# A new order of steps for a windowed-attention and gated-MLP kernel with a hand-written list of steps

## The chip, the core and the metric

The kernel runs on one core of a Trainium2 chip. Such a core has four engines that compute, each with its own queue that is worked off strictly in order: TensorE (PE in the profile; PEld is its loading of weights), VectorE (DVE), ScalarE (ACT) and GpSimd (POOL). SyncE (SP) issues transfers. The engines wait for each other by semaphores. The metric is the device time of one execution in microseconds, lower is better; the time before is the median of 13 runs.

## What is computed

Attention over 4 batches, 8 heads, 768 positions and heads of 64, where a position sees itself, the 127 before it and the first 4 ("sinks"); then a gated MLP with a mixing over positions, and a residual:

```
scores = where(is_sink | in_window, q @ k.T / sqrt(64), -1e9)
x      = softmax(scores) @ v                       # heads side by side: [4, 768, 512]
h      = gelu_tanh(x @ w_in)                       # 512 -> 1024
u, v   = halves of h
v_n    = (v - mean) / sqrt(var + 1e-6) * g_ln
v_s    = einsum('ts,bsd->btd', w_sg, v_n) + b_sg   # mixes positions, 768 x 768
out    = x + (u * v_s) @ w_out                     # 512 -> 512
```

Inputs and output are float32; the kernel computes in bfloat16 and accumulates in float32.

## The kernel before

The whole program is a list of names, `STEPS`. Each name calls a short function that emits the instructions of one step; the loop at the end of the kernel goes through the list under a manual schedule. So **the list is the order of every engine's queue**: an engine gets its instructions in the order in which the steps that use it stand. The waits between engines follow from the data and from the reuse of buffers. A last letter D, A or P says which engine does a step that several could do (VectorE, ScalarE, GpSimd).

```python
        for step in STEPS.split():
            name, *idx = step.split(".")
            done[step] = code[name](*(int(i) if i.isdigit() else i for i in idx))
```

The steps, with b the batch, p the pair of heads (0 to 3), and the lines of the profile:

- **Loads.** LQ, LK, LV (L192, L196, L214) are issued by GpSimd and cast to bfloat16; a batch of q or k comes in 4 parts for batches 0 and 3 and in 2 parts for batches 1 and 2. LW, LWS, LWO are the weights (L233, L237, L240). A buffer of q or k holds two parts (`q16`, `k16`: ring of 2), so that a later load waits until TQ or TK has read the earlier one.
- **Turning q and k.** TQ, TK (L300) turn a pair's q or k on TensorE, 12 transposes on half the array's columns; EQ, EK (L219 on ScalarE, L221 on VectorE) copy the result out of PSUM. For batch 3, EQ and EK are instead transposing transfers issued by SyncE (L310), and XD (L427) does the same with x for batches 2 and 3.
- **Attention.** QK.b.p.g (L350) computes scores of group g of two key tiles (g = 0, 1, 2; the last is smaller), 4 matmuls on half the array's rows; EX (L358, ScalarE) is exp; MK (L365 on VectorE as a product with a mask, L369 and L373 on GpSimd as two selects) masks; KS (L323), SK (L332, L336) and SX (L341) make the sinks' weights. AV.b.p.half (L390, L396, L400) multiplies with v, with a column of ones for the sum; it needs the masks of groups 0 and 1 (half 0) or 1 and 2 (half 1). NR (L409, L410, VectorE) divides by the sum and writes x.
- **MLP.** XT (L419) and XE (L219, L221) turn x; MV (L436) and GV (L440) make the half that is normalised, MU (L478) and GU (L484) the other. BN, RS, NM (L449, L457, L460) are the statistics, Z (L466 on ScalarE, L469 on VectorE) normalises. WT and WE (L491, L494) turn the mixing weights. SP (L499) mixes positions, GT (L504, VectorE) scales and adds the bias, GM (L509 on VectorE or GpSimd) multiplies with u, OU (L516) is the last product, RA (L520) adds x, ST (L523) stores.
- **HM.n** puts n filler matmuls (L180) ahead of the next step on TensorE; they write to the PSUM buffer that this step is about to overwrite.

PSUM is two rings: `sc` of 2 double buffers for QK, MV and MU, and `mm` of 4 for everything else. A step on TensorE thus also waits for the reader of the buffer two or four uses back. The mask step shows how a step chooses its engine:

```python
    def MK(b, p, g, e="D"):
        ...
        if e == "D":
            m = (mask0 if g == 0 else mask1)[:, 0:w]
            nc.vector.tensor_mul(pt[:, :, 0:w], pt[:, :, 0:w],
                                 m.unsqueeze(1).to_broadcast([128, 2, w]))
            return
```

In the list, attention of the next batch is interleaved with the MLP of the one before; the list ends with the MLP of batch 3 alone.

Of the kernel before, what the change touches and what calls it, by code (L numbers as in the profile page):

```python
# [25 lines left out]
WT.3 WE.2 WT.5 GV.0.1 MV.0.2 WE.3 BN.0.0 MU.0.0 GV.0.2 WE.5 BN.0.1 WT.0 GU.0.0 MU.0.1 BN.0.2 RS.0.1 WT.4 GU.0.1 TQ.1.1
TQ.1.0 EQ.1.1.A MU.0.2 LQ.2.0 WE.4 EQ.1.0.A NM.0.1 RS.0.2 WE.0 Z.0.3.A MU.0.3 Z.0.0.D Z.0.1.A NM.0.2 Z.0.4.D Z.0.2.A
TK.1.0 Z.0.5.D WT.1 GU.0.3 EK.1.0.D SP.0.1.0 GU.0.2 WE.1 SP.0.1.2 GT.0.1.0 GM.0.1.0.P QK.1.0.1 GT.0.1.2 QK.1.0.0
TQ.1.2 EX.1.0.1 GM.0.1.2.D TQ.1.3 EQ.1.2.D SP.0.1.3 SP.0.0.2 GT.0.1.3 EQ.1.3.A MK.1.0.1.D TK.1.3 EX.1.0.0 GM.0.1.3.D
TK.1.2 GT.0.0.2 QK.1.0.2 EK.1.2.A SP.0.1.1 EK.1.3.D GM.0.0.2.P EX.1.0.2 QK.1.2.2 MK.1.0.0 SP.0.0.3 EX.1.2.2 MK.1.0.2.D  # L30
GT.0.1.1 QK.1.2.0 QK.1.3.0 GT.0.0.3 EX.1.2.0 TQ.2.0 GM.0.1.1.P TK.1.1 EQ.2.0.D SP.0.0.1 EX.1.3.0 LK.2.0 MK.1.2.0
LV.2.0 EK.1.1.A QK.1.2.1 GM.0.0.3.D QK.1.3.2 OU.0.5 EX.1.2.1 GT.0.0.1 LV.2.1 KS.1.0 OU.0.3 EX.1.3.2 RA.0.5 MK.1.2.1.P
SK.1.0 RA.0.3 ST.0.5 QK.1.3.1 SX.1.0 LQ.2.1 QK.1.1.2 MK.1.3.2.D TQ.2.1 ST.0.3 AV.1.0.1 MK.1.3.0 LK.2.1 EQ.2.1.A
AV.1.0.0 MK.1.2.2.D LV.2.2 AV.1.2.0 NR.1.0.1 EX.1.3.1 AV.1.2.1 NR.1.0.0 GM.0.0.1.P TK.2.1 EX.1.1.2 QK.1.1.0 NR.1.2.1
TK.2.0 MK.1.3.1.P EK.2.1.A QK.1.1.1 NR.1.2.0 EX.1.1.0 LV.2.3 MK.1.1.2.D AV.1.3.1 EX.1.1.1 MK.1.1.0 QK.2.1.2 LQ.3.0
AV.1.3.0 NR.1.3.1 EX.2.1.2 OU.0.4 NR.1.3.0 EK.2.0.A MK.1.1.1.P QK.2.1.1 RA.0.4 QK.2.1.0 EX.2.1.1 XT.1.3 LK.3.0 XT.1.1
ST.0.4 XE.1.3.D AV.1.1.0 EX.2.1.0 TQ.2.3 XE.1.1.D AV.1.1.1 NR.1.1.0 LV.3.0 EQ.2.3.A QK.2.0.2 MK.2.1.0 QK.2.0.1 TQ.2.2
EX.2.0.2 LQ.3.1 NR.1.1.1 TK.2.3 EQ.2.2.A TK.2.2 EK.2.3.D XT.1.2 EK.2.2.A LK.3.1 XT.1.0 XE.1.2.D QK.2.0.0 EX.2.0.1
SP.0.0.0 KS.2.0 LV.3.1 EX.2.0.0 XE.1.0.D SK.2.0 GT.0.0.0 MV.1.0 LQ.3.2 SX.2.0 MK.2.0.0 GM.0.0.0.D EQ.3.0 MK.2.0.1.D
OU.0.1 MK.2.0.2.P GV.1.0 AV.2.0.0 RA.0.1 MK.2.1.2.P MV.1.1 MK.2.1.1.P ST.0.1 EK.3.0 BN.1.0 MV.1.2 GV.1.1 BN.1.1  # L40
AV.2.1.1 GV.1.2 EQ.3.1 OU.0.2 BN.1.2 OU.0.0 RS.1.1 MU.1.3 LK.3.2 EK.3.1 RA.0.0 MU.1.1 NM.1.1 GU.1.3 RA.0.2 LV.3.2
Z.1.3.A Z.1.0.D MU.1.2 NR.2.1.1 RS.1.2 GU.1.1 ST.0.2 ST.0.0 NR.2.0.0 LQ.3.3 MU.1.0 GU.1.2 Z.1.1.D EQ.3.2 NM.1.2
Z.1.2.D LK.3.3 AV.2.0.1 Z.1.4.D GU.1.0 Z.1.5.D QK.2.2.0 AV.2.1.0 NR.2.0.1 EX.2.2.0 LV.3.3 SP.1.1.3 NR.2.1.0 SP.1.0.1
GT.1.1.3 EK.3.2 GM.1.1.3.D QK.2.2.1 GT.1.0.1 QK.2.3.0 SP.1.0.0 EX.2.2.1 MK.2.2.0 GM.1.0.1.P EX.2.3.0 SP.1.1.1 GT.1.0.0
MK.2.2.1.P QK.2.3.1 GT.1.1.1 QK.2.2.2 SP.1.1.0 EX.2.3.1 GM.1.0.0.D EQ.3.3 GM.1.1.1.D MK.2.3.0 EX.2.2.2 AV.2.2.0
QK.2.3.2 MK.2.3.1.D SP.1.0.3 EX.2.3.2 NR.2.2.0 MK.2.2.2.P EK.3.3 AV.2.3.0 GT.1.1.0 QK.3.1.2 QK.3.1.0 GT.1.0.3
GM.1.1.0.P AV.2.2.1 EX.3.1.2 NR.2.3.0 SP.1.1.2 EX.3.1.0 GM.1.0.3.P NR.2.2.1 XD.2.0 QK.3.0.0 MK.2.3.2.D QK.3.0.2
SP.1.0.2 EX.3.0.0 GT.1.1.2 KS.3.0 EX.3.0.2 AV.2.3.1 GT.1.0.2 GM.1.1.2.P SK.3.0 NR.2.3.1 QK.3.0.1 SX.3.0 QK.3.1.1
OU.1.4 MK.3.0.2.D EX.3.0.1 XD.2.1 GM.1.0.2.D MK.3.1.0 OU.1.3 EX.3.1.1 MK.3.0.1.D OU.1.2 MK.3.1.1.D MU.2.1 RA.1.4
RA.1.2 MV.2.0 ST.1.4 RA.1.3 GU.2.1 ST.1.2 MK.3.1.2.D ST.1.3 MK.3.0.0 OU.1.1 GV.2.0 MV.2.1 RA.1.1 BN.2.0 ST.1.1 MV.2.2  # L50
GV.2.1 BN.2.1 MU.2.3 GV.2.2 OU.1.5 BN.2.2 RS.2.1 GU.2.3 OU.1.0 MU.2.0 NM.2.1 RS.2.2 RA.1.0 Z.2.3.A RA.1.5 ST.1.0
MU.2.2 Z.2.2.D GU.2.0 ST.1.5 NM.2.2 Z.2.1.D Z.2.0.D AV.3.1.0 GU.2.2 QK.3.3.2 Z.2.4.D AV.3.1.1 NR.3.1.0 EX.3.3.2
QK.3.3.1 AV.3.0.1 NR.3.1.1 AV.3.0.0 Z.2.5.D NR.3.0.1 SP.2.0.1 EX.3.3.1 MK.3.3.2.D QK.3.2.2 NR.3.0.0 MK.3.3.1.P
QK.3.2.1 SP.2.0.3 EX.3.2.2 GT.2.0.1 EX.3.2.1 MK.3.2.2.P AV.3.3.1 GT.2.0.3 QK.3.2.0 NR.3.3.1 MK.3.2.1.P SP.2.0.0
EX.3.2.0 GM.2.0.3.P AV.3.2.1 GT.2.0.0 QK.3.3.0 GM.2.0.1.P NR.3.2.1 SP.2.1.3 EX.3.3.0 XD.3.1 GM.2.0.0.D SP.2.0.2
MK.3.2.0 GT.2.1.3 AV.3.2.0 MK.3.3.0 SP.2.1.2 GM.2.1.3.P GT.2.0.2 AV.3.3.0 NR.3.2.0 SP.2.1.1 GM.2.0.2.P NR.3.3.0
SP.2.1.0 GT.2.1.2 XD.3.0 GT.2.1.1 GM.2.1.2.P OU.2.1 GT.2.1.0 GM.2.1.1.P MV.3.2 RA.2.1 GM.2.1.0.P OU.2.3 GV.3.2 ST.2.1
OU.2.2 RA.2.3 OU.2.4 ST.2.3 RA.2.2 MV.3.0 BN.3.2 ST.2.2 MV.3.1 RA.2.4 RS.3.2 GV.3.0 ST.2.4 NM.3.2 BN.3.0 Z.3.5.A
MU.3.0 GV.3.1 Z.3.4.A OU.2.0 BN.3.1 GU.3.0 MU.3.2 RA.2.0 RS.3.1 MU.3.1 GU.3.2 ST.2.0 NM.3.1 OU.2.5 Z.3.0.A Z.3.3.D
Z.3.1.D Z.3.2.A MU.3.3 RA.2.5 GU.3.1 ST.2.5 SP.3.1.1 GU.3.3 SP.3.0.1 GT.3.1.1 GM.3.1.1.P SP.3.0.3 GT.3.0.1 GM.3.0.1.D  # L60
SP.3.1.0 GT.3.0.3 GM.3.0.3.D SP.3.0.2 GT.3.1.0 GM.3.1.0.P SP.3.0.0 GT.3.0.2 GM.3.0.2.D SP.3.1.3 GT.3.0.0 GM.3.0.0.P
SP.3.1.2 GT.3.1.3 GM.3.1.3.P OU.3.1 GT.3.1.2 OU.3.0 GM.3.1.2.D RA.3.1 OU.3.3 RA.3.0 ST.3.1 OU.3.4 ST.3.0 RA.3.3 OU.3.5
ST.3.3 OU.3.2 RA.3.5 RA.3.2 ST.3.5 ST.3.2 RA.3.4 ST.3.4
"""


# [506 lines left out]
```

The softmax here doesn't subtract the row's maximum and nothing guards it: scores larger than these inputs give would overflow.

## Time and profile before

| | |
|---|---|
| median of 13 runs | 164.26 us (162.61 to 165.99) |
| profiled execution, device time | 163.6 us |
| its span (first to last instruction) | 161.9 us |
| instructions | 3811 |
| bytes moved by DMA | 22.70 MB, mean 140 GB/s |
| first start of MV.0.0, the MLP's first product | 26.93 us |

The page gives each engine's busy time and share of the span, then the span in 40 slices of about 4 us: a digit is a busy share in tenths, and the row PEclk is the clock that was granted to TensorE, in tenths. The chain is the sequence of work that ended last, followed back from the end. A timeline row reads: start in us, duration in us, engine, line, operation, written tile <- read tiles, for matmuls the part of the array in use (rows*columns), the shape, how many instructions the row merges, and in brackets the idle time before it and what ended it.

### The profile page before, as it was taken

The numbers are of one execution on the slowest core, as the hardware profiler recorded it, in microseconds if no ns is written. First come the engines' busy times: TensorE is split into PE (matmuls) and PEld (weight loads), VectorE is DVE, ScalarE is ACT, GpSimd is POOL, SyncE is SP. The second block draws the span as 40 slices with busy tenths as digits, with TensorE's granted clock in tenths as the row PEclk, the third lists the DMA queues.
The fourth block names the chain that finished last, engine by engine and source line by source line (L and its number), as shares of the span: only waits on it lengthen the run. The fifth ranks groups of instructions, "written<-read, shape, count | busy, mean of one in ns | idle before, by whom it ended". The sixth has DMA issues, their size and how long they took to land.

```text
span 161.9 us, 3811 instructions
## 1 busy us (share of the span) xinstructions
PE 149.9 (93%) x1521; PEld 87.4 (54%) x1521; DVE 131.7 (81%) x305; ACT 100.3 (62%) x117; POOL 88.8 (55%) x119
## 2 busy tenths in 40 slices
PE   4869798999999979999999999999999999999980
PEld 1426565566655556744565565545756644556530
DVE  4468999599899998967999999879988948857761
ACT  3377994749978789994278768545886024770000
POOL 7999984425225999998894861004076731204400
PEclk9996999999999999999999999999999999999997
DMA  5999999999970999999999955810301654030055
GB/s 163 170 156 176 195 210 209 204 221 180 176 104 0 128 235 193 192 155 143 174 222 204 156 102 109 248 65 0 134 0 36 97 130 184 10 132 0 4 196 194
DMA packets 63122, 22.70 MB, mean 140 GB/s; under 512 B 51456, under 2 KB 59904, under 8 KB 63104
## 3 DMA queue, kind: packets, MB, share of 16 engines
q0 software_dynamic: 45600, 11.80, 74.3%
q1 hardware_dynamic: 17504, 10.66, 26.6%
q8 instruction: 12, 0.20, 0.5%
q14 instruction: 6, 0.05, 0.1%
HBM read 24.81 MB, written 6.29 MB: 192 GB/s over the span
## 4 chain that ended last, share of the span: by engine, by line
PE 77%; DVE 6%; POOL 5%; ACT 4%; DMA 3%; issue 1%; DVEq 0%; POOLq 0%
PE mm L499 19%; PE mm L516 13%; PE sc L478 13%; PE sc L436 11%; PE sc L350 6%; PE mm L300 4%; DMA q<-in_q_dram 3%; PE mm L390 3%; DVE x_sb L410 3%; ACT P L358 3%; PE mm L396 2%; DVE P L365 2%; PE mm L400 2%; PE mm L491 1%; PE mm L419 1%; POOL P L369 1%
## 5 line engine op out<-in xcount | busy, mean ns | idle before, releaser
L358 ACT ACTIVATE P<-sc 128x1024 bf16<-128x1024 f32 (+1 forms) x48 | 43.9, 963 | 8.1 <-PE sc L350 7.6
L499 PE MATMUL mm<-wsgT,z 128*128 128x384 bf16 x192 | 34.4, 327 | 0.0
L509 POOL TENSOR_TENSOR wsg_gated<-gtmp,uT 128x384 bf16<-128x384 bf16 x19 | 17.8, 950 | 22.9 <-DVE gtmp L504 19.5
L499 PEld LDWEIGHTS <-z 128*128 128x128 bf16 x192 | 17.5, 98 | 12.1 <-issue 1.8
L504 DVE SCALAR_TENSOR_TENSOR gtmp<-mm,g_sb,b_bc 128x384 bf16<-128x384 f32 x32 | 19.4, 613 | 5.6 <-PE mm L499 5.6
L440 ACT ACTIVATE vt<-sc 128x1024 f32<-128x1024 f32 x12 | 12.3, 1023 | 17.0 <-PE sc L436 17.0
L516 PE MATMUL mm<-w_out_sb,wsg_gated 128*128 128x512 bf16 x96 | 22.7, 379 | 0.0
L478 PE MATMUL sc<-xT,w_in_sb 128*128 128x384 bf16 x128 | 22.4, 326 | 0.0
L436 PE MATMUL sc<-w_in_sb,xT 128*128 128x512 bf16 x96 | 22.0, 379 | 0.0
L457 POOL TENSOR_TENSOR rs<-rs,neg_half 128x4 f32<-128x4 f32 (+1 forms) x8 | 7.1, 886 | 26.4 <-DVE rs L452 25.6
L520 DVE TENSOR_TENSOR ot<-mm,x_sb 128x512 f32<-128x512 f32 x24 | 16.2, 689 | 6.3 <-PE mm L516 6.2
L365 DVE TENSOR_TENSOR P<-P,mask 128x1024 bf16<-128x1024 bf16 (+1 forms) x32 | 20.6, 670 | 0.2
L214 POOL DMA_DIRECT2D v_sb<-in_v_dram x16 | 16.9, 1060 | 4.8 <-DMA wsg_gated<-in_moe_w_sg_dram 3.5
L410 DVE TENSOR_TENSOR x_sb<-mm,rcp 128x384 bf16<-128x384 f32 x32 | 17.8, 558 | 1.1
L390 PE MATMUL mm<-v_sb,P 128*128 128x65 bf16 x192 | 17.6, 197 | 0.9 <-DVE x_sb L410 0.5
L484 ACT ACTIVATE uT<-sc 128x768 bf16<-128x768 f32 x16 | 12.8, 806 | 8.2 <-PE sc L478 8.2
L449 DVE BATCH_NORM_STATS2 st<-vt 128x6 f32<-128x512 f32 x24 | 16.2, 674 | 1.6 <-ACT vt L440 1.6
L390 PEld LDWEIGHTS <-P 128*128 128x128 bf16 x192 | 15.0, 100 | 4.5 <-issue 1.8
L478 PEld LDWEIGHTS <-w_in_sb 128*128 128x128 bf16 x128 | 12.4, 98 | 9.0
L350 PE MATMUL sc<-qT,kT 64*128 64x256 bf16 x192 | 15.9, 269 | 1.2 <-DVE x_sb L410 0.9
L396 PE MATMUL mm<-v_sb,P 128*128 128x65 bf16 x160 | 16.3, 197 | 0.2 <-POOL P L373 0.2
L369 POOL TENSOR_SCALAR_AFFINE_SELECT P<-P 128x512 bf16<-128x512 bf16 x16 | 11.1, 695 | 7.4 <-ACT P L358 7.4
(73 smaller groups left out, 227.4 us busy)
## 6 DMA issues: line engine op xcount, KB each, us to landing
out_dram<-ot SPq DMA_DIRECT2D x24, 256.0 KB, 2.2
v_sb<-in_v_dram POOLq DMA_DIRECT2D x16, 192.0 KB, 8.1
q<-in_q_dram POOLq DMA_DIRECT2D x4, 384.0 KB, 13.0
k<-in_k_dram POOLq DMA_DIRECT2D x4, 384.0 KB, 13.6
wsg_gated<-in_moe_w_sg_dram POOLq DMA_DIRECT2D x1, 1152.0 KB, 12.6
w_in_sb<-in_moe_w_in_dram POOLq DMA_DIRECT2D x2, 512.0 KB, 8.0
qn<-in_q_dram POOLq DMA_DIRECT2D x8, 96.0 KB, 7.4
kn<-in_k_dram POOLq DMA_DIRECT2D x8, 96.0 KB, 6.2
```

Of the source, the lines that this page charges most:

```text
L350: nc.tensor.matmul(sc[:, hl, 256 * jl:256 * jl + n], kT[b, p][rows, 128 * j:128 * (j + 1)], qT[b, p][rows, 128 * j:128 * j + n], start=Tru ...
L358: nc.scalar.activation(out=pt[:, :, 0:w], in_=sc_ring[b, p, g][:, :, 0:w], func=AF.Exp, scale=scale)
L365: nc.vector.tensor_mul(pt[:, :, 0:w], pt[:, :, 0:w], m.unsqueeze(1).to_broadcast([128, 2, w]))
L390: nc.tensor.matmul(av[:, il, hl, :], P[b, p, i // 2][:, hl, 256 * (i % 2):256 * (i % 2) + 128], vb[:, h, i, :], start=first, stop=False)
L396: nc.tensor.matmul(av[:, il, hl, :], P[b, p, j // 2][:, hl, 256 * (j % 2) + 128:256 * (j % 2) + 256], vb[:, h, j, :], start=False, stop=False)
L410: nc.vector.tensor_mul(xs[:, 3 * half:3 * half + 3, 128 * p:128 * (p + 1)].rearrange("p t (h d) -> p t h d", h=2), av[:, :, :, 0:Dh], rcp. ...
L436: nc.tensor.matmul(hp[:, jl, :], xT[b][:, j, c, :], w_in_sb[:, c, d_half:2 * d_half], start=(c == 0), stop=(c == KD - 1))
L478: nc.tensor.matmul(hp[:, n, 0:NH], w_in_sb[:, c, 128 * dc:128 * (dc + 1)], xT[b][:, 3 * hf:3 * hf + 3, c, :], start=(c == 0), stop=(c == K ...
L499: nc.tensor.matmul(ps[:, 0:NH], z[b][:, si, 128 * dc:128 * (dc + 1)], wsgT[:, si, NH * hf:NH * (hf + 1)], start=(si == 0), stop=(si == NT ...
L504: nc.vector.scalar_tensor_tensor(out=gtmp.new((b, hf, dc)), in0=mm_ring["g", b, hf, dc][:, 0:NH], scalar=g_sb[:, dc:dc + 1], in1=b_bc[:, N ...
L509: (nc.vector if e == "D" else nc.gpsimd).tensor_mul(gatedT[:, (2 * b + hf) % 3, dc, :], gtmp[b, hf, dc], uT[b][:, dc, NH * hf:NH * (hf + 1)])
L516: nc.tensor.matmul(ps, gatedT[:, (2 * b + hf) % 3, dc, 128 * tl:128 * (tl + 1)], w_out_sb[:, dc, :], start=(dc == 0), stop=(dc == KU - 1))
```

## The change

Nothing but the list `STEPS` differs. Every step other than HM is in both lists, in a new order, and the last letter of 51 steps is another. Letters by engine, before and after:

| step | before | after |
|---|---|---|
| MK on GpSimd / VectorE | 16 / 32 | 20 / 28 |
| GM on GpSimd / VectorE | 19 / 13 | 15 / 17 |
| Z on ScalarE / VectorE | 9 / 15 | 11 / 13 |
| EQ, EK on ScalarE / VectorE | 14 / 10 | 12 / 12 |
| XE on ScalarE / VectorE | 3 / 5 | 4 / 4 |
| filler matmuls (HM) | 13 in 4 places | 11 in 5 places |

The list was planned with GpSimd taken to go first when it and VectorE want the port to SBUF that the two share; nothing in the code sets this. The loads and what turns q, k and x in which batch are as before.

The diff, cut to the parts that are spoken of (start, batch 1, the passage into batch 2, end):

```diff
-LK.0.2 TK.0.0 LV.0.1 EK.0.0.A TQ.0.1 QK.0.0.2 KS.0.0 LQ.0.3 EQ.0.1.D QK.0.0.1 EX.0.0.2 SK.0.0 LK.0.3 VSM.0 TK.0.1
-LV.0.2 EK.0.1.D SX.0.0 QK.0.0.0 MK.0.0.2.P EX.0.0.1 HM.1 TQ.0.2 KS.0.1 LV.0.3 EX.0.0.0 QK.0.1.2 EQ.0.2.D SK.0.1
-MK.0.0.1.P TK.0.2 EX.0.1.2 QK.0.1.1 EK.0.2.D SX.0.1 QK.0.1.0 LW.0 AV.0.0.1 EX.0.1.1 MK.0.0.0 LW.1 KS.0.2 EX.0.1.0 HM.1
-AV.0.0.0 NR.0.0.1 QK.0.2.2 SK.0.2 MK.0.1.1.P NR.0.0.0 EX.0.2.2 TQ.0.3 TK.0.3 SX.0.2 QK.0.2.1 LWS MK.0.1.0 EQ.0.3.A
-QK.0.2.0 EK.0.3.D AV.0.1.0 EX.0.2.1 MK.0.2.2.P NR.0.1.0 EX.0.2.0 LWO QK.0.3.1 MK.0.2.1.D XT.0.0 EX.0.3.1 KS.0.3 LQ.1.0
-QK.0.3.0 MK.0.2.0 SK.0.3 AV.0.2.1 XE.0.0.A LK.1.0 MK.0.1.2.D AV.0.2.0 NR.0.2.1 SX.0.3 MK.0.3.1.P QK.0.3.2 AV.0.1.1
-EX.0.3.0 NR.0.2.0 LV.1.0 NR.0.1.1 EX.0.3.2 MK.0.3.0 LV.1.1 HM.4 XT.0.2 MK.0.3.2.D XE.0.2.A AV.0.3.0 LQ.1.1 AV.0.3.1
-NR.0.3.0 LK.1.1 NR.0.3.1 XT.0.1 LV.1.2 XE.0.1.D XT.0.3 VSM.1 MV.0.0 XE.0.3.A LV.1.3 VSM.3 VSM.2 MV.0.1 GV.0.0 LG WT.2
...
-TQ.1.0 EQ.1.1.A MU.0.2 LQ.2.0 WE.4 EQ.1.0.A NM.0.1 RS.0.2 WE.0 Z.0.3.A MU.0.3 Z.0.0.D Z.0.1.A NM.0.2 Z.0.4.D Z.0.2.A
-TK.1.0 Z.0.5.D WT.1 GU.0.3 EK.1.0.D SP.0.1.0 GU.0.2 WE.1 SP.0.1.2 GT.0.1.0 GM.0.1.0.P QK.1.0.1 GT.0.1.2 QK.1.0.0
...
-AV.1.0.0 MK.1.2.2.D LV.2.2 AV.1.2.0 NR.1.0.1 EX.1.3.1 AV.1.2.1 NR.1.0.0 GM.0.0.1.P TK.2.1 EX.1.1.2 QK.1.1.0 NR.1.2.1
...
-SP.3.1.2 GT.3.1.3 GM.3.1.3.P OU.3.1 GT.3.1.2 OU.3.0 GM.3.1.2.D RA.3.1 OU.3.3 RA.3.0 ST.3.1 OU.3.4 ST.3.0 RA.3.3 OU.3.5
-ST.3.3 OU.3.2 RA.3.5 RA.3.2 ST.3.5 ST.3.2 RA.3.4 ST.3.4
+EQ.0.0.A TK.0.0 LV.0.1 EK.0.0.A TQ.0.1 KS.0.0 QK.0.0.2 LQ.0.3 EQ.0.1.D QK.0.0.0 EX.0.0.2 SK.0.0 LK.0.3 VSM.0 TK.0.1
+LV.0.2 EK.0.1.D SX.0.0 QK.0.0.1 MK.0.0.2.P EX.0.0.0 HM.1 TQ.0.2 KS.0.1 LV.0.3 EX.0.0.1 MK.0.0.0 SK.0.1 QK.0.1.2 LW.0
+TK.0.2 EQ.0.2.D SX.0.1 QK.0.1.1 EX.0.1.2 EK.0.2.D MK.0.0.1.P EX.0.1.1 QK.0.1.0 MK.0.1.2.D LW.1 HM.1 AV.0.0.0 EX.0.1.0
+KS.0.2 QK.0.2.1 MK.0.1.1.D TQ.0.3 LWS EX.0.2.1 QK.0.2.0 MK.0.1.0 AV.0.1.1 LWO EX.0.2.0 NR.0.0.0 AV.0.1.0 QK.0.2.2
+NR.0.1.1 TK.0.3 EQ.0.3.A MK.0.2.1.P NR.0.1.0 EK.0.3.A SK.0.2 LQ.1.0 AV.0.0.1 MK.0.2.0 SX.0.2 XT.0.0 KS.0.3 LK.1.0
+EX.0.2.2 NR.0.0.1 QK.0.3.0 AV.0.2.0 LV.1.0 EX.0.3.0 XE.0.0.D QK.0.3.1 XT.0.2 MK.0.2.2.D EX.0.3.1 SK.0.3 LV.1.1
+MK.0.3.0 QK.0.3.2 AV.0.2.1 NR.0.2.0 SX.0.3 MK.0.3.1.P EX.0.3.2 NR.0.2.1 XE.0.2.A LQ.1.1 MK.0.3.2.D HM.1 AV.0.3.0
+NR.0.3.0 LK.1.1 AV.0.3.1 LV.1.2 NR.0.3.1 XT.0.1 XE.0.1.A HM.1 XT.0.3 LV.1.3 XE.0.3.D MV.0.0 VSM.1 VSM.3 MV.0.2 GV.0.0
...
+MU.0.0 NM.0.2 RS.0.1 WE.1 Z.0.5.A WE.2 Z.0.4.A TQ.1.1 WE.4 TQ.1.0 NM.0.1 GU.0.0 WE.5 TK.1.0 LQ.2.0 MU.0.1 Z.0.3.D
...
+TK.1.1 EX.1.3.2 QK.1.3.0 MK.1.0.0 LK.2.0 SP.0.1.1 EK.1.1.A MK.1.3.2.D LV.2.0 EX.1.3.0 KS.1.0 QK.1.1.0 TQ.2.1 LV.2.1
+GT.0.1.1 EX.1.1.0 TQ.2.0 SK.1.0 MK.1.3.0 QK.1.1.2 LQ.2.1 SX.1.0 QK.1.2.2 EQ.2.1.D SP.0.0.0 EX.1.1.2 GM.0.0.2.P
...
+AV.1.2.1 EX.1.2.0 NR.1.3.0 MK.1.1.1.P TQ.2.3 NR.1.2.1 EX.2.1.1 TQ.2.2 QK.2.1.2 GM.0.0.0.P EQ.2.3.D AV.1.1.0 EQ.2.2.A
...
+SP.3.1.3 GT.3.1.2 GM.3.1.2.D OU.3.1 GT.3.1.3 OU.3.2 GM.3.1.3.P RA.3.1 OU.3.0 ST.3.1 RA.3.2 OU.3.4 ST.3.2 RA.3.0 OU.3.3
+ST.3.0 OU.3.5 RA.3.3 ST.3.3 RA.3.5 ST.3.5 RA.3.4 ST.3.4
```

## The prediction, made before the changed kernel was run

> **What bounds the kernel now.** I read the page first (busy shares, slices, chain), then the chain in order of time, then TensorE's timeline matmul by matmul, and last the other engines' timelines where TensorE waits.
>
> ```profile
> PE 149.9 (93%) x1521; PEld 87.4 (54%) x1521; DVE 131.7 (81%) x305; ACT 100.3 (62%) x117; POOL 88.8 (55%) x119
> ...
> PEclk9996999999999999999999999999999999999997
> ...
> PE 77%; DVE 6%; POOL 5%; ACT 4%; DMA 3%; issue 1%; DVEq 0%; POOLq 0%
> ```
>
> TensorE carries 77% of the chain that ended last. A busy share of 93% is not work, since matmuls overlap and their ends are modelled; so I count starts. The chain in order of time gives what a step costs when nothing stands in its way:
>
> ```profile
> 31.55 1.73 PE sc L436 x8
> 33.28 1.30 PE sc L478 x8
> ...
> 144.27 7.80 PE mm L499 x48
> 152.07 5.19 PE mm L516 x24
> ```
>
> So MV costs 1.73 us, MU 1.30, SP 7.80/8 = 0.98, OU 5.19/6 = 0.86. From starts in the timeline a transposing step (TQ, TK, XT, WT) costs 0.34, QK 0.22 (0.17 for its third group), AV 0.35 or 0.53, SK 0.22. The next rows show a surcharge:
>
> ```profile
> 46.21 0.86 PE L300 MATMUL mm<-iden,k 128*64 128x128 bf16 x24
> 47.00 0.34 PE L350 MATMUL sc<-qT,kT 64*128 64x256 bf16 x4
> 47.27 1.15 PE L499 MATMUL mm<-wsgT,z 128*128 128x384 bf16 x6
> 48.36 0.34 PE L350 MATMUL sc<-qT,kT 64*128 64x256 bf16 x4
> ```
>
> SP from 47.27 to 48.36 takes 1.09 instead of 0.98. The same 0.09 to 0.12 appears wherever the tile of the array changes (64*128 for QK, 128*64 for TQ and TK, 128*128 for the rest, 128*32 for later SK), and never between equal ones: 0.10 us a change. Now TensorE's span divides:
> - until MV.0.0 starts: 26.93 us, for 13.7 us of work and 23 changes (2.3);
> - from there to the end of OU.3.2 at 157.09: 130.16 us. Work: 12 MV 20.8, 16 MU 20.8, 32 SP 31.4, 24 OU 20.7, 12 pairs of AV 10.6, 36 QK 7.3, TQ and TK 5.4, WT and XT 3.4, SK 0.7, together 120.9; 64 changes 6.4; waits are the rest, 2.9;
> - after it 4.8 us: two RA and the last store.
>
> The 2.9 us lie in few places. The largest:
>
> ```profile
> 57.67 0.20 PE L390 MATMUL mm<-v_sb,P 128*128 128x65 bf16 x1 [0.34 <-DVE P L365]
> ...
> 60.45 0.19 PE L390 MATMUL mm<-v_sb,P 128*128 128x65 bf16 x1 [0.45 <-DVE x_sb L410]
> ```
> ```profile
> 55.16 2.46 DVE L365 TENSOR_TENSOR P<-P,mask 128x768 bf16<-128x768 bf16 x3
> ```
>
> AV.1.2.1 and AV.1.3.1 start some 0.7 and 0.5 us late. VectorE was still masking: three masks took 2.46 us; by their rows (two of 0.69, here one of 0.68, and two of 0.55) they should take 1.7. Further waits are 0.4 us at AV.2.1.1 (76.0, for a GpSimd mask), and 0.2 to 0.3 at SK.3.0, QK.3.2.2 and AV.3.2.1.
>
> **The change, part by part.** No work goes away except two filler matmuls (13 to 11), both ahead of MV.0.0.
>
> *Changes of tile.* Counted along the two lists after MV.0.0: 64 before, 58 after; 6 x 0.10 = 0.6 us less. Nothing hides this, since TensorE itself is the chain there. Ahead of MV.0.0 it is 25 instead of 23, inside idle time.
>
> *The start.* Both lists run alike until q of the third head pair lands at 11.3 us. There the clock is also low: slice 4 shows 0.6 after a stretch in which TensorE mostly waited. The old ScalarE queue then lost time:
>
> ```profile
> 16.51 0.81 ACT L358 ACTIVATE P<-sc 128x768 bf16<-128x768 f32 x1 [1.19 <-PE sc L350]
> ```
>
> QK.0.2.2 stood behind both AV.0.0.1 and AV.0.0.0, which waited for GpSimd's mask. The new list puts one AV ahead of QK.0.2.1 and moves EK.0.3 from VectorE (0.875) to ScalarE (0.69). Queue by queue, with start-to-start times from the rows (EX 0.92, third group 0.71, SX 0.48, copies 0.69; GpSimd mask 1.18 in full; load issues 0.72 to 1.01):
> - GpSimd: MK.0.0.2 ends at 11.6 as now; LV 1.0, LW.0 0.8, MK.0.0.1 1.2 give 14.5; LW.1, LWS, LWO 2.4; MK.0.2.1 1.2; four loads 3.5: free at 21.5.
> - ScalarE: EX.0.1.0 ends at 15.3 as now; EX.0.2.1 starts at 15.55 when AV.0.0.0 has let QK.0.2.1 through; EX.0.2.0 to 17.4; EQ.0.3, EK.0.3, SX.0.2, EX.0.2.2, EX.0.3.0, EX.0.3.1 (0.69+0.69+0.48+0.71+0.92+0.92) to 21.8.
> - So MK.0.3.1 runs 21.9 to 23.1, AV.0.3.0 starts at 23.2 (now 24.53), NR.0.3.0 ends 24.4, XT.0.1 24.8, XE.0.1 on ScalarE (0.68 against VectorE's 0.47, +0.2) 25.8. MV.0.0 gets through at 25.9: 1.0 us earlier. Bounds: 0.7 us later than now if a half-clock window of 3.4 us falls on MV (1.7 lost), 1.5 us earlier if XE's halves overlap as they do now.
>
> *What is late next: the loads.* The software queue moves packets without a break from 4 to 44 us, so issuing earlier hardly lands earlier. k of batch 1 was issued at 19.86 and landed 18.0 us later, at 37.9 (the slowest k load shows as 18.6). The old list needs it at 39.97; the new one puts TK.1.0 right behind TQ.1.0, at 27.3 us of TensorE's own work, which with the earlier start is 37.4. It waits 0.5 us. Likewise for TQ.2.3: from the issue of LK.2.0 to the landing of LQ.2.1 passed 11.9 us (51.42 to 63.36), and the new list leaves about 11.5 (LK.2.0 follows TK.1.1, some 37.7 us into TensorE's own work; TQ.2.3 stands at 49.2): 0.3 us. Both bounds reach from 0 to 1 us.
>
> *Waits by queue.* For every step that TensorE takes from another engine I added up that engine's queue from its last release, against TensorE's work in between. The old list falls short by 0.56 at AV.1.3.1 (NR.1.2.0, eight entries of VectorE behind RA.0.3), 0.7 at AV.1.1.0 (MK.1.1.1, nine of GpSimd), 0.65 at XT.1.3 (EK.2.0, seven of ScalarE), 0.43 at AV.2.1.1: there the trace has its waits. In the new list no step falls short by over 0.06; the closest are QK.1.2.2, MV.1.2 and AV.3.3.1. As the old sums explain about 2 of 2.9 us, I leave 1.0 us for the new list.
>
> *Moves between engines.* 4 masks go from VectorE to GpSimd (4 x 0.60 off, 4 x 1.18 on), 4 gate products back (4 x 0.28 on, 4 x 0.87 off), 2 normalisations and a copy to ScalarE, and copies of q back to VectorE: VectorE -1, ScalarE +1, GpSimd +1 us in all, beside TensorE's work; they cost nothing, and where cover ends is in the sums above. SP's stores and transposes keep their order of need; XD.3.0 is issued near 111 us of work and lands after 3.6, ahead of MU.3.1 at 116.4.
>
> *The shared port.* The code sets no priority; the list only plans with one. Rows: VectorE masks of 1024 that lie wholly inside GpSimd work take 0.68 to 0.69 like those that meet none; one of 32 stretched, by 0.84 (at 55.2), three normalisations by 0.36 to 0.54 while GpSimd issued loads (80 to 85), and a few GpSimd operations by 0.2 to 0.5: some 4 us in all, mostly hidden. The Trainium skill, "SBUF — State Buffer", section "SBUF: two separate sides", states an exclusive lock: a VectorE instruction with two SBUF inputs and a GpSimd one that reads SBUF never overlap, and the loser waits in full. By the rule four more GpSimd masks would cost up to 4 x 1.2 = 4.8 us of VectorE delay; by the rows, a stretch of 0.84 in one of 32, 0.1. I take the row, and keep the rule for the slow rival.
>
> **Sum.** MV.0.0 at 25.9, work 120.9, changes 5.8, waits 0.5 + 0.3 + 1.0 = 1.8, end 4.8: 159.2 us of span against 161.9, or -2.7. The profiled execution took 163.6 (1.7 around its span), 0.7 below the median; from the median 164.26 - 2.7 = 161.6.
>
> **Rivals.**
> - *Forecast*, 161.6 (own range 160.2 to 162.9), 0.62.
> - *The waits come back elsewhere.* For: the largest old wait was a stretched mask that no sum shows, and the new list has as many steps with under 0.35 us to spare (26 against 34). Then waits are 2.9 and the late loads on top 0.4: 163.1. Against: the planned shortfalls are gone. 0.18.
> - *Loads rule batches 1 and 2.* The start's gain is lost at TK.1.0, and TQ.2.3 waits 1 us: 162.8. For: the unbroken queue. 0.06.
> - *GpSimd's masks become the bound (slower).* Place: MK.1.0.2 to MK.2.1.2, eight GpSimd masks between GpSimd's loads, at 45 to 75 us, where TensorE has only short steps. Price: a collision, 0.5 to 0.8 us each on either side. It decides from 2.7 us, four or five collisions on the path; at eight, +5 less 1 of slack: 165.6. For: the lock rule, and the list plans GpSimd first. Against: one such collision in that stretch now. 0.14.
>
> From 0.5% (0.8 us; about what a measurement here can tell): faster 0.71, same 0.15, slower 0.14. The range, 160.0 to 164.6, leaves out the far part of the slow rival and a start that gains over 2 us.
>
> **What would show it.** MV.0.0 at 25.9 in TensorE's timeline; a wait for k in front of TK.1.0; AV.1.2.1, AV.1.3.1 and AV.2.1.1 without waits; VectorE's masks at 0.69 and GpSimd's at 0.70. I am wrong if MV.0.0 starts after 27, if the clock row shows a low slice after 24 us, or if VectorE's or GpSimd's mean mask is longer by 0.1 us.

## The result, and the profile after

| | before | after |
|---|---|---|
| median | 164.12 us (48 runs) | 161.43 us (11 runs, 160.66 to 164.53) |
| ratio, 95% interval | | 0.9874 [0.9838, 0.9910] |
| profiled execution, device time | 163.6 us | 160.66 us |
| its span | 161.9 us | 159.0 us |
| start of MV.0.0 | 26.93 us | 25.18 us |

The new order is faster by 1.3% (0.9 to 1.6%), that is 2.1 us (1.5 to 2.7). The ratio leaves out runs over 1.5% above the fastest of their kernel; the medians of the table do not, and they differ by 2.7. The page of the changed kernel, the rows that answer to those of before:

```profile
PE 147.8 (93%) x1519; PEld 86.2 (54%) x1519; DVE 131.6 (83%) x304; ACT 100.7 (63%) x118; POOL 88.6 (56%) x123
...
PEclk9999999999999999999999999999999999999998
...
PE 78%; DMA 9%; POOL 9%; DVE 1%; issue 0%; POOLq 0%
```

TensorE still carries the end, and the busy times of the other engines moved by at most 0.4 us. Two things differ. The clock row has lost its 6 in the fourth slice. And the chain runs through DMA for 9%, where it had DVE 6% and ACT 4%: something now waits for a load. TensorE's timeline shows it:

```profile
25.83 2.97 PE L436 MATMUL sc<-w_in_sb,xT 128*128 128x512 bf16 x13
29.61 0.84 PE L491 MATMUL mm<-iden,wsg_gated 128*128 128x128 bf16 x12 [0.81 <-DMA wsg_gated<-in_moe_w_sg_dram]
```

WT.3, the first step that turns the mixing weights, stands behind two MV and waits until w_sg has landed, at 29.56. By starts of steps the wait is 0.97 us, longer than the bracket, since the matmuls' modelled ends cover part of the gap. The place where the old list had its largest wait is clean. TensorE's timeline around the step AV.1.3.1 (57.83) and AV.1.2.1 (59.56):

```profile
57.03 0.86 PE L300 MATMUL mm<-iden,k 128*64 128x128 bf16 x24
57.83 0.20 PE L390 MATMUL mm<-v_sb,P 128*128 128x65 bf16 x1
...
58.94 0.61 PE L350 MATMUL sc<-qT,kT 64*128 64x256 bf16 x8
59.56 0.20 PE L390 MATMUL mm<-v_sb,P 128*128 128x65 bf16 x1
```

No row has a bracket. But the mask that AV.1.2.1 needs took long again. VectorE's timeline just before:

```profile
57.42 2.08 DVE L365 TENSOR_TENSOR P<-P,mask 128x1024 bf16<-128x1024 bf16 x2
```

Two masks of 0.69 took 2.08 and ended at 59.50, 0.06 ahead of the matmul. In the old list such a stretch cost 0.7 us; in the new one the step stands far enough back that it cost nothing, with nothing to spare.

The division of the span that the prediction made, in both profiled executions:

| stretch | before | after | change |
|---|---|---|---|
| until MV.0.0 | 26.93 | 25.18 | -1.75 |
| changes of tile after it, x 0.10 | 64 | 58 | -0.6 |
| waits after it | 2.88 | 2.29 (0.97 of it for w_sg) | -0.6 |
| after OU.3.2 or its successor | 4.81 | 4.81 | 0 |

### The profile page after: what moved, and what is told of

The parts are those of the page before. It is cut to its first block, busy times and chain, and to the rows that moved or that the text cites. A ratio compares the mean times of both kernels' runs of the same rounds, so it can differ in the third digit from the quotient of the medians.

```text
span 159.0 us, 3815 instructions
## 1 busy us (share of the span) xinstructions
PE 147.8 (93%) x1519; PEld 86.2 (54%) x1519; DVE 131.6 (83%) x304; ACT 100.7 (63%) x118; POOL 88.6 (56%) x123
## 4 chain that ended last, share of the span: by engine, by line
PE 78%; DMA 9%; POOL 9%; DVE 1%; issue 0%; POOLq 0%
PE mm L499 20%; PE sc L478 13%; PE mm L516 13%; PE sc L436 11%; DMA wsg_gated<-in_moe_w_sg_dram 9%; PE sc L350 6%; PE mm L300 4%; PE mm L390 3%; POOL v_sb L214 2%; PE mm L396 2%; PE mm L400 2%; POOL q L192 1%; PE mm L491 1%; POOL k L192 1%; PE mm L419 1%; POOL w_in_sb L233 1%
## 5 line engine op out<-in xcount | busy, mean ns | idle before, releaser
L509 POOL TENSOR_TENSOR wsg_gated<-gtmp,uT 128x384 bf16<-128x384 bf16 x15 | 14.1, 948 | 16.9 <-DVE gtmp L504 15.8
L478 PE MATMUL sc<-xT,w_in_sb 128*128 128x384 bf16 x128 | 23.1, 326 | 0.0
L369 POOL TENSOR_SCALAR_AFFINE_SELECT P<-P 128x512 bf16<-128x512 bf16 x20 | 13.3, 666 | 15.1 <-ACT P L358 15.0
L390 PE MATMUL mm<-v_sb,P 128*128 128x65 bf16 x192 | 16.9, 194 | 0.7 <-ACT xT L219 0.6
L390 PEld LDWEIGHTS <-P 128*128 128x128 bf16 x192 | 14.5, 98 | 4.5 <-issue 2.4
L457 POOL TENSOR_TENSOR rs<-rs,neg_half 128x2 f32<-128x2 f32 (+1 forms) x8 | 7.0, 875 | 17.5 <-DVE rs L452 14.9
L396 PE MATMUL mm<-v_sb,P 128*128 128x65 bf16 x160 | 15.8, 194 | 0.0
```

The source lines that it names most:

```text
L390: nc.tensor.matmul(av[:, il, hl, :], P[b, p, i // 2][:, hl, 256 * (i % 2):256 * (i % 2) + 128], vb[:, h, i, :], start=first, stop=False)
L396: nc.tensor.matmul(av[:, il, hl, :], P[b, p, j // 2][:, hl, 256 * (j % 2) + 128:256 * (j % 2) + 256], vb[:, h, j, :], start=False, stop=False)
L478: nc.tensor.matmul(hp[:, n, 0:NH], w_in_sb[:, c, 128 * dc:128 * (dc + 1)], xT[b][:, 3 * hf:3 * hf + 3, c, :], start=(c == 0), stop=(c == K ...
```

## Experiments

The theory after the result: about 0.8 us comes from the start (with the wait for w_sg taken off), about 2.2 from fewer changes of tile and fewer waits after MV.0.0, and the new letters (which engine does a step) cost nothing and bring nothing. Rivals: all of the gain is the start, where the half-clock stretch happened to be missing; or the gain needs the letters. Ratios are to the kernel before on the same chip.

**The new start with the old rest, and the reverse.** Cut at MV.0.0, each part with its own letters:

```diff
 (e1)  steps up to XE.0.3: new list;  MV.0.0 and all behind it: old list
 (e2)  steps up to MV.0.0: old list;  all behind it: new list
```

> New list up to MV.0.0, then the remaining steps in the order and with the letters of the old list. Theory (the start is 1.75 us shorter in the new profile, but about 1.0 us of it is waited back at the first WT step for w_sg, whose transfer lands no earlier; the rest of the gain is made behind MV.0.0): MV.0.0 near 25.2, a wait of about 1 us at WT.2, in all 0.8 us faster than before (ratio 0.995). Rival (the start is the whole gain): 1.75 us or more faster, ratio 0.989 or less.

> Old list up to MV.0.0, then the remaining steps as in the new list. Theory: the first WT step finds w_sg landed, since MV.0.0 starts near 26.9; six changes of tile less (0.6 us) and 1.6 us of waits less: 2.2 us faster than before, ratio 0.9865, about as fast as the whole new list. Rival (the start is the gain): 0.6 to 1.1 us faster, ratio 0.993 to 0.997.

Measured: e1 0.9944 [0.9906, 0.9981], e2 0.9891 [0.9834, 0.9947]. The start alone brings 0.9 us (0.3 to 1.5), the rest alone 1.8 (0.9 to 2.7). The sum, 2.7, is above the 2.1 of the whole list, within these intervals. The first rival falls: it needed a ratio of 0.989 or less in e1. e1 has 64 changes of tile and 3.54 us of waits behind MV.0.0, e2 58 and 2.07. In e1 the old waits are back, in the old places:

```profile
57.13 0.21 PE L390 MATMUL mm<-v_sb,P 128*128 128x65 bf16 x1 [0.46 <-DVE P L365]
57.83 0.53 PE L300 MATMUL mm<-iden,k 128*64 128x128 bf16 x12 [0.16 <-DVE x_sb L410]
59.91 0.19 PE L390 MATMUL mm<-v_sb,P 128*128 128x65 bf16 x1 [0.45 <-DVE x_sb L410]
```

One expectation failed: no wait for w_sg in e1. It landed at 29.62 and WT.2 stood at 29.72, so it was close; the q loads had landed 1.1 us later in this execution and the start with them (MV.0.0 at 26.27).

**The load of w_sg ahead of the second half of w_in.**

```diff
-... MK.0.1.2.D LW.1 HM.1 AV.0.0.0 ... TQ.0.3 LWS EX.0.2.1
+... MK.0.1.2.D LWS LW.1 HM.1 AV.0.0.0 ... TQ.0.3 EX.0.2.1
```

> New list with LWS (w_sg) issued ahead of LW.1 instead of behind it, nothing else. Theory (TensorE waits 0.97 us at WT.3 for w_sg, which lies behind the 512 KB of LW.1 in one queue): w_sg lands 2 to 3 us earlier, the wait is gone, TK.1.0 then waits up to 0.4 us for k, which lands as before near 37.1: 0.6 us faster than the new list, ratio 0.984. Rival (all loads of the start share a queue that never empties, so what waits is only moved): the same ratio as the new list, 0.987.

Measured: 0.9887 [0.9844, 0.9930], no gain over the changed kernel. The load landed at 27.12, 2.4 us earlier than in the first profile, as expected. But here q landed at 12.25 and MV.0.0 began at 27.41: the start was too late for w_sg to matter either way. So not every execution pays the 0.97 us. Whether one does depends on when w_sg lands (28.95 to 31.10 in the 11 profiles with LWS behind LW.1) as much as on the start: in e4a, below, MV.0.0 began at 26.20, w_sg landed at 30.61, and WT.3 waited 1.00 us.

**The changed kernel once more**, to see whether the early start was chance:

> The new list once more, beside the others on one chip. Its start decides which theory of the start holds. Theory: MV.0.0 stands 14.2 us behind the landing of q of the third pair where no half-clock window falls between 10 and 24 us (and WT.3 then waits 0.5 to 1 us for w_sg), 15.0 to 15.2 us where one does (and WT.3 waits for nothing); ratio 0.985 to 0.991. Rival (order alone): 13.9 to 14.3 us in either case.

Measured: 161.22 us, 0.9884 [0.9849, 0.9919]. Span 159.4; q landed at 11.74, MV.0.0 began at 25.94, 14.20 us behind it, as in the first profile. WT.3 found w_sg landed (29.17) and did not wait, so the expectation of 0.5 to 1 us there missed. Instead SP.1.1.3, the first mixing product of batch 1, waited 0.89 us by starts for VectorE's Z:

```profile
82.20 0.49 PE L499 MATMUL mm<-wsgT,z 128*128 128x384 bf16 x2
83.41 1.31 PE L499 MATMUL mm<-wsgT,z 128*128 128x384 bf16 x7 [0.72 <-DVE z L469]
```

**More filler matmuls ahead of TQ.0.2**, to hold the clock up, in the old list (e4) and in the new one (e4a):

```diff
-HM.1 TQ.0.2
+HM.6 TQ.0.2
```

> Old list, with 6 filler matmuls instead of 1 ahead of TQ.0.2, where TensorE waits over 1 us for q in any case. Theory (most of the start's 1.75 us in the new profile is not the order but the clock: the old profile has a window of 3.4 us at half clock from 13.4 us on, the new one none): no half-clock window, MV.0.0 about 1.0 us earlier relative to the landing of that q (14.6 instead of 15.6 us behind it), time 0.6 us or more below before, ratio 0.993 to 0.996. Rival (order alone makes the start): the half-clock window stays or costs nothing, ratio 1.000.

> New list with the same 6 fillers ahead of TQ.0.2. Theory (the clock's window, where it falls, costs the start 1 us, and part of that is waited back for w_sg): MV.0.0 14.2 us behind the landing of q of the third pair, full clock, as in the new profile; time at or up to 0.5 us below the new list, ratio 0.984 to 0.988. Rival (fillers delay TQ.0.2): ratio 0.990.

Measured: e4 0.9999 [0.9935, 1.0062], e4a 0.9839 [0.9780, 0.9899]. In the old list the stretch at half clock did not go, it moved. By stretches of time, with TensorE's busy time first and PEclk as the number behind POOL; first before, then e4:

```profile
13.00:14.00 1.00, 1.00 (x12) 0.49 (x9) 0.96 (x2) 1.00 (x3) 1.00 (x3) 0.55 1.37 194
14.00:15.00 1.00, 1.00 (x15) 0.90 (x14) 1.00 (x2) 1.00 (x2) 1.00 (x2) 0.50 2.01 169
...
17.00:20.00 3.00, 2.15 (x51) 1.55 (x46) 2.71 (x5) 3.00 (x5) 2.85 (x6) 1.00 1.37 203
```

```profile
13.00:15.00 2.00, 2.00 (x37) 1.28 (x36) 1.84 (x3) 2.00 (x3) 2.00 (x4) 1.00 1.71 183
15.00:17.00 2.00, 1.68 (x35) 1.09 (x36) 1.93 (x6) 1.82 (x3) 1.98 (x4) 1.00 2.27 165
17.00:20.00 3.00, 1.64 (x37) 1.03 (x31) 2.97 (x5) 3.00 (x5) 2.99 (x6) 1.00 1.35 200
20.00:24.00 4.00, 3.86 (x45) 2.38 (x41) 3.52 (x9) 3.37 (x5) 3.12 (x4) 0.62 1.21 209
```

Before ran at half clock from 13.10 to 16.51; e4 kept full speed there, but between 17 and 20 TensorE was busy for 1.64 of 3 us, and the half clock came behind that, from 20.96 to 24.37. MV.0.0 began 16.7 us behind the landing of q, where 14.6 was expected and before has 15.6. The ratio rests on five of the 12 runs of e4, at 162.6 to 164.8 us; the other seven, the profiled one among them, took 165.4 to 166.4. So e4 does not tell what full clock through the whole start would bring to the old list, and its median of all runs, 165.40, gives no reason to use it. e4a's interval overlaps that of the changed kernel: no difference shown, and its profile has no half-clock stretch, like the changed kernel's two without the fillers. How often the stretch falls is counted below.

**The old letters in the new order**: all 51 (e5), the 12 of MK alone (e7), the 39 others alone (e7b). Of the diff:

```diff
 (e5, e7)   -MK.1.0.2.P ... MK.1.2.2.P ... MK.1.2.1.D
            +MK.1.0.2.D ... MK.1.2.2.D ... MK.1.2.1.P
 (e5, e7b)  -EK.0.3.A ... XE.0.0.D XE.0.1.A
            +EK.0.3.D ... XE.0.0.A XE.0.1.D
```

> New order, but every step on the engine that the old list gave it. Theory (order decides; the moves between engines are hidden): within 0.6 us of the new list, ratio 0.984 to 0.992. Rival (the letters relieve the queues that made TensorE wait, so order and letters only work together): 1.5 us or more slower than the new list, ratio 0.997 or more, with new waits of TensorE in batch 1.

> New order and new letters, but each MK on the engine that the old list gave it (16 instead of 20 on GpSimd, others swapped). All letters back cost 5.4 us against the new list. Theory (the letters of the masks are the ones that fit the order, since a mask stands between EX and AV with little to spare): ratio 1.000 or more, half or more of that loss, with waits at AV in batches 1 and 2. Rival (copies and gate products matter more: EQ, EK, XE, GM, Z): ratio below 0.994.

> New order with the new letters of the masks, but the old letters of EQ, EK, XE, Z and GM. All letters back: ratio 1.020; the masks alone: 1.000. Theory (the losses add, as they lie on different waits): about 1.007, that is 3.3 us slower than the new list, with waits at SP.0.1.0 or TQ.1.0 (Z, EQ) and none at AV.1.1.0. Rival (masks and copies hinder each other in one VectorE queue): 0.995 or less.

Measured: e5 1.0204 [1.0161, 1.0248], e7 0.9995 [0.9958, 1.0032], e7b 1.0026 [0.9988, 1.0064]. Against 0.987 to 0.989 of the changed kernel the masks' letters are worth some 1.2%, 2 us, the others' 1.4%, 2.3 us, and all together 3.2%, over 5 us. The theory that the letters cost and bring nothing falls: the new order with the old letters is slower than before. All three keep the 58 changes of tile; what grows is the waits after MV.0.0, to 5.37, 3.41 and 4.30 us against 2.0 to 2.3, and in e5 also the start: 15.5 us lie between the landing of q and MV.0.0, where the changed kernel has 14.2 at the same full clock. (e7's profile has a half-clock stretch and 15.4 us.) The reverse, the new letters in the old order, was not run; so it is shown that the new order needs its letters, not what the letters would bring without it. The waits of e7b, from TensorE's timeline:

```profile
38.17 0.53 PE L300 MATMUL mm<-iden,k 128*64 128x128 bf16 x12 [0.39 <-DVE wsgT L494]
41.25 1.96 PE L499 MATMUL mm<-wsgT,z 128*128 128x384 bf16 x11 [0.40 <-ACT z L466]
55.01 0.40 PE L350 MATMUL sc<-qT,kT 64*128 64x256 bf16 x4 [0.31 <-ACT P L358]
65.26 0.34 PE L350 MATMUL sc<-qT,kT 64*128 64x256 bf16 x4 [0.22 <-ACT P L358]
85.33 1.80 PE L499 MATMUL mm<-wsgT,z 128*128 128x384 bf16 x10 [0.51 <-DVE z L469]
```

And those of e7, which e7b does not have:

```profile
62.84 0.20 PE L390 MATMUL mm<-v_sb,P 128*128 128x65 bf16 x1 [0.25 <-POOL P L369]
63.42 0.20 PE L396 MATMUL mm<-v_sb,P 128*128 128x65 bf16 x1 [0.20 <-POOL P L373]
```

Each looks like an entry put into a queue that had no room for it, which was not tested one by one. In e7, MK.1.2.1 goes to GpSimd directly ahead of MK.1.1.1; AV.1.1.0 stands behind both and waits. In e7b, ScalarE and VectorE trade entries, and SP.0.1.0 waits for Z. The sizes of e7 and e7b (2.0 + 2.3) come near e5's 5.3; a remainder of about 1 us stays unassigned, and e7b lost 1 us less than the 3.3 that were expected.

**Two loads moved behind Z.** The steps Z of batch 1 run on VectorE while GpSimd issues k and v of batch 3. e6 puts these issues behind the first gate product:

```diff
-AV.2.1.0 LK.3.3 Z.1.2.D ... NR.2.1.1 LV.3.3 SP.1.1.1 ... GM.1.1.3.P QK.2.3.1
+AV.2.1.0 Z.1.2.D ... NR.2.1.1 SP.1.1.1 ... GM.1.1.3.P LK.3.3 LV.3.3 QK.2.3.1
```

> New list with LK.3.3 and LV.3.3 put behind GM.1.1.3.P on GpSimd, so that GpSimd issues no loads while VectorE normalises batch 1. Theory ([...]three Z took 2.68 us instead of 1.5 in two of the runs, and SP.1.1.3 waited 0.89 us): Z back at 0.54 us each, no wait at SP.1.1.3, 0.1 to 0.9 us faster than the new list, ratio 0.982 to 0.986. Rival (the stretch has another cause): Z as long as before, same ratio 0.987.

Measured: 0.9825 [0.9760, 0.9890]. The wait at SP.1.1.3, 0.89 us in four of the five profiles that have this order and these letters behind MV.0.0 and the loads in place (0.13 in the first), is gone. The three Z, first in e3 (loads in place), with GpSimd at the same time, then in e6:

```profile
82.15 2.68 DVE L469 TENSOR_SCALAR z<-vt,rs,nmr 128x512 bf16<-128x512 f32 x3
```

```profile
81.84 1.72 POOL L196 DMA_DIRECT2D kn<-in_k_dram  x2
83.54 1.04 POOL L214 DMA_DIRECT2D v_sb<-in_v_dram  x1
```

```profile
81.31 1.46 DVE L469 TENSOR_SCALAR z<-vt,rs,nmr 128x512 bf16<-128x512 f32 x3
```

The same three instructions take 2.68 us beside load issues and 1.46 without. (In the first profile, where the issue of v began 0.11 us before they ended, they took 1.91, and the wait was 0.13.) So it is the load issues that stretch Z, and this stretch is the wait at SP.1.1.3; the gain in time, about 0.5%, lies within the intervals.

**All edits that helped, together.** e8 is e3, e4a and e6 in one; e9 also issues LWO only ahead of MV.0.0, so that k of batch 1 lands earlier:

```diff
-MK.0.1.0 AV.0.1.1 LWO EX.0.2.0 ... XT.0.3 LV.1.3 XE.0.3.D
+MK.0.1.0 AV.0.1.1 EX.0.2.0 ... XT.0.3 LV.1.3 LWO XE.0.3.D
```

> New list with the three edits that were tried one at a time: 6 fillers ahead of TQ.0.2, LWS ahead of LW.1, LK.3.3 and LV.3.3 behind GM.1.1.3.P. Theory (they remove different waits: the half-clock window, then the wait for w_sg that an earlier start meets, then the stretched Z): MV.0.0 14.2 us behind the landing of q of the third pair, no wait at WT.3 and SP.1.1.3, TK.1.0 up to 0.7 us for k: 1.0 to 1.8 us below the new list of the same chip, ratio to before 0.976 to 0.982. Rival (the earlier start only meets k of batch 1 in the same queue): all but the Z is waited back, 0.9 us below the new list at most.

> As e8, and LWO (512 KB of w_out, first needed by OU.0 after 50 us) put behind LV.1.3. Theory (the loads share one queue that is never empty up to 44 us): k of batch 1 lands 2.5 us earlier, near 35, so that TK.1.0 waits for nothing: another 0 to 0.7 us, ratio 0.974 to 0.980. Rival (TK.1.0 did not wait in e8): the same as e8.

Measured: e8 160.53 us, 0.9844 [0.9793, 0.9896], with the shortest span of all, 158.3; e9 160.25 us, 0.9815 [0.9762, 0.9868], span 159.5. Neither waits for w_sg nor at SP.1.1.3; waits after MV.0.0 are 1.43 and 1.78. On the same chip the changed kernel had 161.22, so e8 is lower by 0.7 us and e9 by 1.0, 0.6%. Both ratios miss what was expected (0.976 to 0.982 and 0.974 to 0.980). e9 has the lowest median, but the intervals overlap. In e8 k landed at 36.90 and TK.1.0 began at 36.95: that load was on the edge. e9's k landed at 34.66.

**How often the half clock falls.** The profiles are single executions, but the mean granted clock of every execution in these experiments is on record. One stretch of 3.41 us at 0.50 takes 0.011 off it, and the executions fall into two groups, up to 0.990 and from 0.992. The profiles that have the stretch lie in the first group, those without it in the second. Counted so (an estimate, since a stretch at the very end of the kernel lowers the mean too), the old list had the stretch in 19 of 65 executions and the new one in 8 of 24. Side by side, from the run in which the changed kernel was timed once more:

| median | before | changed kernel |
|---|---|---|
| clock 0.992 or more | 162.83 us (17 executions) | 161.17 us (9) |
| clock up to 0.990 | 164.18 us (6) | 162.33 us (3) |

The stretch costs 1.2 to 1.4 us here, it falls about as often in both lists, and the new list is faster by 1.7 to 1.9 us in each group. So the rival that the gain is a missing half-clock stretch falls for the medians, though it holds in part for the two profiles that were compared first. On e1's chip the executions at 0.992 or more give 162.56 for e1 (9) and 163.57 before (13): the start brings 1.0 us at equal clock. The six fillers do what they were for in the new list: e4a, e8 and e9 have none at 0.990 or below, of 18. In the old list they do not: e4 has six of 12.

## Why the prediction held, step by step

- **Total.** 161.6 forecast, 161.43 measured; span 159.2 against 159.0. The route holds, and e1 and e2 split the gain as the sum did: 1.0 for the start (measured 0.9), 1.7 for the rest (measured 1.8). That the totals meet to 0.2 us is luck in part: the ratio makes the gain 2.1 us, and the 2.7 of the forecast is the edge of its interval; the profile of span 159.0 is that of the fastest of the table's 11 runs (the second has 159.4). The nine items of work as shown add to 121.1, not 120.9; SP was rounded up.
- **Start.** MV.0.0 forecast at 25.9, found at 25.18 and 25.94. In the second profile each station fits: MK.0.3.1 22.1 to 23.4 (21.9 to 23.1 forecast), NR.0.3.0 ends 24.6 (24.4), MV.0.0 25.94. The first profile is 0.76 us ahead of the second from EX.0.1.0 (14.00 against 14.75) on, and so is the landing of q of the third pair (10.98 against 11.74). Over 14 executions it landed between 10.97 and 12.51, and the start moves with it; no sum over the queues can hold that.
- **The clock.** Measured from that landing, MV.0.0 comes 14.2 to 14.4 us later in all six profiles that have the new start with its letters and no half-clock stretch, 14.9 to 15.2 in the two with one (e3, e6), and 15.55 to 15.62 in the old start with one (before, e2). So of the 1.75 us between the profiles of before and after about 0.3 is q's landing, 0.5 the order at equal clock, and 0.7 to 1 a half-clock stretch that did not fall there. That MV.0.0 stood where the forecast had it in these profiles, though the forecast gave the queues all of its 1.0 us, is thus half luck. Over all executions the stretch is no part of the gain, and the start's 0.9 to 1.0 us in e1 is what the queues were said to bring; whether that or the 0.5 of these profiles is nearer stays open.
- **Changes of tile.** 64 to 58, as counted, and e1 and e2 carry the counts with the halves. No run changes the number of changes alone, but the traces bear the size out: behind MV.0.0 in before, in both profiles of the changed kernel and in e6, 238 pairs of steps on unlike tiles lie 0.10 us further apart than the first step's own time (median), 450 pairs on like tiles 0.00. With 0.10 us for each change, 0.5 to 1.0 us of the waits of every profile lie in pieces under 0.12 us, which have no name.
- **Waits for loads.** Forecast 0.5 at TK.1.0 and 0.3 at TQ.2.3; both were nothing. k landed at 37.05 against the forecast 37.9, ahead of TK.1.0 at 37.71, and q at 59.84 against 60.20. In their place came 0.97 us for w_sg, which the forecast had not looked at: a start that comes early meets the next load in the same queue. The step was right in kind (loads bound an early start), wrong in the load. The two errors nearly cancel, by luck; the second profile has neither wait.
- **Other waits.** 1.0 forecast, 1.3 found in the first profile, none over 0.24 us by starts. AV.1.3.1, AV.1.2.1 and AV.2.1.1 do not wait. But the second profile found 2.0, with 0.89 of it at SP.1.1.3, and e2, e3 and e4a have this wait too: the queue sums had Z at its length alone, and load issues stretch it. Of the rival of returning waits, the words "as many steps" do not fit its own counts, 26 against 34.
- **"Moves between engines cost nothing."** True of the new list as a whole, where the letters fit the order; false as a general statement, as e5, e7 and e7b show (2 to 5 us). The forecast's queue sums included the new letters, so its number was not hurt.
- **The shared port.** This step was too low. VectorE's mean mask, before and after, which I had named as a sign that I would be wrong:

```profile
L365 DVE TENSOR_TENSOR P<-P,mask 128x1024 bf16<-128x1024 bf16 x22 | 14.9, 686 | 0.2
```

```profile
L365 DVE TENSOR_TENSOR P<-P,mask 128x1024 bf16<-128x1024 bf16 x21 | 16.3, 793 | 0.3 <-ACT P L358 0.2
...
L369 POOL TENSOR_SCALAR_AFFINE_SELECT P<-P 128x512 bf16<-128x512 bf16 x20 | 13.3, 666 | 15.1 <-ACT P L358 15.0
```

It grew by 0.107 us: five of 21 were stretched, to 1.04, 1.08, 1.11, 1.12 and 1.40, some 2.3 us in sum where 0.1 was forecast. GpSimd's selects were not (666 against 695 ns). The slow rival thus had its collisions, but few of them, and in this profile on steps that could bear them: AV.1.2.1 took two stretched masks with 0.06 us left. "Mostly hidden" was too good all the same: the stretched Z cost 0.89 us of TensorE's time at SP.1.1.3 in four of the five profiles, which e6 took away.

## What to carry to other kernels

An order of steps and the choice of engines are one plan: the new order without its letters was slower than the old list. Compare executions at the same granted clock before a difference between two profiles is put down to the change. When a start is moved forward, look for the next load in the same queue, not only for the one that is known to be late. Keep load issues on GpSimd away from VectorE work that reads only SBUF, unless that work has 0.5 us to spare.

## What the runs showed of the hardware

**Which VectorE work is stretched beside GpSimd.** Over all 14 profiles, 128x1024 masks (two SBUF inputs), by what GpSimd did in the same time:

| GpSimd meanwhile | masks | over 0.85 us | mean |
|---|---|---|---|
| nothing, or selects, or small work | 84 | 0 | 0.684 us |
| of these: selects | 17 | 0 | 0.681 us |
| issuing a load | 177 | 45 | 0.785 us |
| gate product (128x384), no load | 38 | 16 | 0.917 us |

Z (one SBUF tensor, float32 to bfloat16) takes 0.54 us alone, 104 times, and 0.765 on average where it begins while GpSimd issues a load; 42 of these 63 exceed 0.62. VectorE's gate products (two SBUF inputs, 0.354 alone) do stretch beside selects: 24 of 47 exceed 0.45.

The order in which the two begin parts these numbers further. Of the 128x1024 masks, Z and gate products of VectorE that began before the GpSimd instruction that they met, none of 58 was stretched; all that were stretched began while GpSimd was at work. The other way round, GpSimd's 32 gate products that began while VectorE was in a mask or gate product took 1.19 us on average, none under 1.00, and the other 198 took 0.92. So where one of these waits, it is the one that began second. What reads PSUM never did: NR takes 0.557 us beside load issues, beside GpSimd's computing and beside nothing. GpSimd's issues of v take 1.04 us whether VectorE does such work or not. The Trainium skill, "SBUF — State Buffer", section "Who interferes with whom", says that a VectorE instruction with at most one SBUF input, outside certain fast modes, does not contend, which NR bears out (whether Z ran in such a mode no run shows), and that one with two contends with GpSimd instructions that read SBUF, whichever is issued first holding the lock and the other waiting in full. The order above agrees with that. What does not agree: of the 17 masks beside selects alone 14 had begun first, but the three that began inside a select were not stretched either, nor were 17 of 41 gate products. The same section has load issues on GpSimd starved by VectorE; here VectorE was the one that lost, 32 of 136 masks among load issues alone. What picks those that are stretched from those that begin second stays open.

**The clock.** A half-clock stretch between 10 and 24 us shows in 6 of 14 profiles: one in the old list (and in e2 with its start), in e3, e6 and e7, and later in e4. It is always 3.413 us long at 0.50. In each profile the starts of the clock's records lie whole multiples of 3.413 us apart, so they mark a grid of windows. Between the first record and 28 us, the six windows that end where a half-clock stretch begins have TensorE busy for 0.66 to 1.96 us of 3.41; the 72 others have 2.03 or more. Busy time is not all that counts: at the end of the kernel four windows with 1.44 to 1.76 us were not followed by half clock at once. The Trainium skill, "TensorE: Matmul & The Clock Gate", section "What's actually happening", states windows of that length that run free of the kernel, which fits, and puts the drop behind an idle window; in these runs a window with up to 1.96 us of work had the same effect. In e1 two windows share the pause ahead of TQ.0.2 (2.19 and 2.09 us busy) and no stretch follows; in e2 one window holds it (0.66). The list does not set where the grid lies, and the changed kernel had the stretch in 8 of 24 executions. That fits chance of phase; it was not tested by itself.
